# ScalarE's share of magnitudes and scales in an attention and two-layer kernel: sums for v, layer 2's magnitude, one factor folded

## The chip, the cores and the metric

The kernel runs on one core of a Trainium2 chip. The metric is the device time of one execution in microseconds (us), the median of the runs; lower is better.

## The reference

Four batches of eight heads (sequence 576, head size 64) go through a masked softmax attention; its output is a 2304 x 512 matrix x, which passes through two dense layers, each with its own pair of weights (512 x 2048 and 2048 x 512):

```python
scores = np.where(masks, scale * q @ k.T, -1e9)      # heads 0-3: a band of 32; heads 4-7: every 32nd
x = softmax(scores) @ v                              # 2304 x 512
h = x @ moe_w_in;  g = np.maximum(0.01 * h, h);      x = g @ moe_w_out
h = x @ moe2_w_in; g = np.maximum(h, 0) + np.log1p(np.exp(-np.abs(h)))
return g @ moe2_w_out
```

The weights arrive as 64-bit floats and are turned into numbers on the chip.

## The kernel before

Every operand of a dense product is split into two f16 parts, a high part and what is left of it, and one product becomes three matmuls (`mm3`, L453 to L456). To be split, a matrix is scaled by a power of two that comes from a bound of its magnitude. So each weight quarter runs through a chain: load (SP's DMA queue, L147), magnitude (`largest`, VectorE, L156), spread over the partitions (`over`, one TensorE product, L122), factors (`scale`, VectorE), integer work on the two words (`low` L162, `sign` L198, VectorE), `shift` (ScalarE, L204), `merge` (VectorE, L209), `high` (ScalarE, L219) and `rest` (L224, GpSimd or VectorE). For w_out of layer 1 (`plan_together`) one more ScalarE pass, `fold` (L216), multiplies the merged quarter by its factor `by` before the split.

Attention works batch by batch in six halves. `dots` (L314) makes scores, `top` finds their maxima (VectorE, L331 for batch 0, L337 otherwise), `expo` (ScalarE, L360) the exponentials with their sums, `guard` and `norm` (L368 to L377) the reciprocals, `spread` (GpSimd, L382) multiplies, `turn` (L391) transposes, `fetch` (ScalarE, L399) copies out of PSUM, `pv` (L411) multiplies by v, and `high` and `rest` (L439 to L450) write x as two f16 parts. The scale of x comes from `largest` over v (VectorE, L257) with `over` and `factor`.

Layer 1 runs over eight token groups of 288: `gate1` makes h in PSUM (L454 to L456), ScalarE bends and splits it (L475, L478), GpSimd makes the rest (L481), and w_out follows. Layer 2 runs over nine groups (`Unit`) of 256 tokens and eight k each. For each k, `first` makes h; `size` takes its magnitude by clearing the sign bit (VectorE, L1124); `relu` (ScalarE, L1131) reads the same h and frees its PSUM bank; `soft` is an exponential with the scale `nsc` and a logarithm (ScalarE, L1138, L1139); `add` joins them (GpSimd, L1143); `sums` (VectorE, L1151), `cut_high` (ScalarE, L1155) and `cut_rest` (VectorE, L1159) make the operands of `second`.

The order on each engine is not written out. Steps are given to `Plan` with an engine, an estimated cost, what they depend on, the buffers that they take and free, and a rank; `Plan.run` lets each engine take, among the steps that can start within 0.5 us of the earliest, the one of smallest rank. `RANKS` holds two numbers for each kind of step: an offset and a slope. Each engine works through its own list in order, SP's queue of loads too. Up to 130 us of planned time, `Plan` fills planned holes of TensorE with products that nobody reads (`idle`, L92, "fillers" below), which keep the engine active.

Of the kernel before, what the change touches and what calls it, by code (L numbers as in the profile page):

```python
# [9 lines left out]
BF16 = mybir.dt.bfloat16  # L10
F16 = mybir.dt.float16
F32 = mybir.dt.float32
I32 = mybir.dt.int32
U32 = mybir.dt.uint32
U16 = mybir.dt.uint16
AF = mybir.ActivationFunctionType
# [4 lines left out]
P = 128  # L21
# [34 lines left out]
def build(tc, qt, kl, ks, v, wi1, wo1, wi2, wo2, mloc, mstr, out):  # L56
    nc = tc.nc
    with ExitStack() as ctx:
# [82 lines left out]
        class Weight:  # L141
# [73 lines left out]
            def fold(self, q, by):  # L215
                nc.scalar.activation(self.f[q], self.f[q], AF.Copy, scale=by)  # L216

            def high(self, q, hl):
                nc.scalar.activation(flat(hl[0]), self.f[q], AF.Copy)  # L219
                self.hl[q] = hl  # L220

            def rest(self, q, eng):
                hi, lo = self.hl[q]
                eng.tensor_tensor(out=flat(lo), in0=self.f[q], in1=flat(hi), op=ALU.subtract)  # L224

# [6 lines left out]
        class Attn:  # L232
# [22 lines left out]
            def largest(self):  # L255
# [3 lines left out]
                )  # L259

# [378 lines left out]
        def plan_attention(A, ld, after=(), behind=(), scaled=()):  # L639
# [8 lines left out]
            big = step("DVE", 3.05, lambda half: A.largest(), [ld["v"]], 1)  # L648
# [43 lines left out]
        def plan_together(W, name, after, parts, then, w1):  # L692
# [28 lines left out]
            for q in range(4):  # L721
                y = step("ACT", 2.07, lambda q=q: W.shift(q, st["s"]), [t] + read[q], 4 + q)
                y = step("DVE", 2.2, lambda q=q: W.merge(q), [y], 4 + q, port=True)
                y = step("ACT", 1.8, lambda q=q: W.fold(q, O1.by[:, q : q + 1]), [y], 4 + q)
                y = step("ACT", 1.85, lambda q=q: W.high(q, parts(q)), [y] + made[-1:] * (q % 2), 4 + q)
# [602 lines left out]
```

## Time and profile before

| | |
|---|---|
| median of 3 runs | 862.68 us (861.14 to 863.2) |
| the profiled execution, its own time | 861.51 us |
| its span in the trace | 859.7 us |
| mean granted clock of TensorE | 0.995 |
| busy: TensorE, VectorE, ScalarE, GpSimd | 834.1, 552.7, 499.7, 289.4 us |

Busy time counts the fillers for TensorE. What the kernel can win is TensorE's time without a product that counts: its idle time, its fillers, and products at the lower clock. A number like "L257" is a line of the kernel before; lines of the changed kernel are some 19 to 24 higher past line 260.

### The profile page before, as it was taken

The page shows a single profiled execution, that of the slowest core. Times are in us where ns is not written, and L with a number is a line of the kernel's source. Part 1 is how long each engine was busy: PE and PEld are TensorE (multiplying, and loading weights), DVE is VectorE, ACT ScalarE, POOL GpSimd, SP SyncE. Part 2 cuts the span into 40 slices and gives each one's busy share as a digit, 9 for nine tenths or more (in the row PEclk, how much of TensorE's full clock was granted, in tenths as well). Part 3 has the DMA queues.
Part 4 walks back from the last instruction along what each step waited for, and adds up shares of the span by engine and source line. Part 5 has one row for each costly group of instructions (what it writes and reads, how often), then busy time and mean ns, then how long its engine had stood idle before and what let it go on. Part 6 is the DMA issues. An engine that isn't in the chain of part 4 may idle for free.

```text
span 859.7 us, 17683 instructions
## 1 busy us (share of the span) xinstructions
PE 834.1 (97%) x7353; PEld 686.2 (80%) x7353; DVE 552.7 (64%) x1236; ACT 499.7 (58%) x934; POOL 289.4 (34%) x198
## 2 busy tenths in 40 slices
PE   9979999999999999999999999999999999999997
PEld 5547677778777777788877787888888888888886
DVE  4999794534305360038757869877787878776675
ACT  4766969835655241354626367556575656566573
POOL 2457747702242041221605033313222322222131
PEclk9989999999999999999999999999999999999999
DMA  9833320231104540022221120000000000000000
GB/s 369 360 111 128 143 99 1 75 131 57 43 17 181 197 196 2 1 98 100 98 99 29 70 99 1 25 2 27 1 26 1 26 1 26 25 2 25 2 25 26
DMA packets 10992, 63.28 MB, mean 74 GB/s; under 512 B 1344, under 2 KB 1440, under 8 KB 7840
## 3 DMA queue, kind: packets, MB, share of 16 engines
q1 hardware_dynamic: 10656, 62.00, 19.1%
q8 instruction: 57, 0.93, 0.4%
q14 instruction: 23, 0.19, 0.1%
q10 hardware_dynamic: 256, 0.16, 0.1%
HBM read 57.44 MB, written 4.72 MB: 72 GB/s over the span
## 4 chain that ended last, share of the span: by engine, by line
PE 63%; DVE 18%; ACT 7%; DMA 5%; issue 4%; POOL 3%; DVEq 0%; POOLq 0%; ACTq 0%
PE h L454 10%; PE h L456 10%; PE h L455 10%; PE o L454 10%; PE o L456 10%; PE o L455 10%; DMA pair<-wo_dram 3%; DVE pair L198 3%; DVE gr L1159 2%; ACT pair L204 2%; PE ps L314 2%; DVE pair L162 2%; POOL w L224 2%; DVE pair L209 2%; DVE m L156 1%
## 5 line engine op out<-in xcount | busy, mean ns | idle before, releaser
L456 PE MATMUL h<-x,w 128*128 128x256 f16 (+1 forms) x1088 | 304.4, 280 | 6.6 <-POOL w L224 6.6
L454 PE MATMUL h<-x,w 128*128 128x256 f16 (+1 forms) x1088 | 304.5, 280 | 4.6 <-ACT t L475 1.9
L455 PE MATMUL h<-x,w 128*128 128x256 f16 (+1 forms) x1088 | 304.4, 280 | 0.0
L1143 POOL TENSOR_TENSOR pair<-pair,t 128x512 f32<-128x512 f32 x72 | 98.8, 1372 | 271.4 <-ACT t L1139 173.6
L481 POOL TENSOR_TENSOR g<-t,g 128x576 f16<-128x576 f32 x64 | 105.1, 1648 | 159.7 <-ACT g L478 159.6
L456 PE MATMUL o<-g,pair 128*128 128x288 f16 x512 | 146.4, 286 | 0.4 <-POOL pair L224 0.3
L454 PE MATMUL o<-g,pair 128*128 128x288 f16 x512 | 146.5, 286 | 0.0
L455 PE MATMUL o<-g,pair 128*128 128x288 f16 x512 | 146.4, 286 | 0.0
L456 PEld LDWEIGHTS <-w 128*128 128x128 f16 x1088 | 106.8, 98 | 26.7 <-POOL w L224 7.2
L455 PEld LDWEIGHTS <-w 128*128 128x128 f16 x1088 | 106.8, 98 | 23.9 <-issue 4.8
L454 PEld LDWEIGHTS <-w 128*128 128x128 f16 x1088 | 106.8, 98 | 21.2 <-ACT w L219 1.0
L1155 ACT ACTIVATE gr<-pair,x2b 128x896 f16<-128x896 f32 x72 | 73.9, 1040 | 63.6 <-DVE pair L1151 63.6
L1159 DVE SCALAR_TENSOR_TENSOR gr<-pair,x2b,gr 128x896 f16<-128x896 f32 x72 | 86.4, 1211 | 27.4 <-ACT gr L1155 26.9
L1151 DVE TENSOR_TENSOR pair<-pair 128x128 f32<-128x128 f32 x288 | 78.3, 316 | 20.2 <-POOL pair L1143 17.7
L382 POOL TENSOR_TENSOR s<-s,sm 96x512 f32<-96x512 f32 (+3 forms) x48 | 49.7, 1055 | 113.4 <-DVE sm L377 72.5
L1131 ACT ACTIVATE pair<-h,x2s 128x512 f32<-128x512 f32 x72 | 49.1, 682 | 60.3 <-DVE t L1124 57.5
L454 PE MATMUL o<-w,gr 128*128 128x256 f16 x306 | 83.4, 273 | 0.0
L456 PE MATMUL o<-w,gr 128*128 128x256 f16 x306 | 83.4, 273 | 0.0
L455 PE MATMUL o<-w,gr 128*128 128x256 f16 x306 | 83.4, 273 | 0.0
L475 ACT ACTIVATE t<-h,gs 128x576 f32<-128x576 f32 x64 | 47.2, 737 | 59.8 <-PE h L456 59.8
L1124 DVE TENSOR_SCALAR t<-h 128x512 int32<-128x512 int32 x72 | 49.2, 685 | 32.0 <-PE h L456 31.3
L456 PEld LDWEIGHTS <-pair 128*128 128x128 f16 x512 | 50.0, 98 | 13.8 <-POOL pair L224 1.2
(123 smaller groups left out, 1396.5 us busy)
## 6 DMA issues: line engine op xcount, KB each, us to landing
pair<-wo_dram SPq DMA_DIRECT2D x12, 2048.0 KB, 7.8
pair<-wi_dram SPq DMA_DIRECT2D x8, 2048.0 KB, 11.0
out_dram<-pair SPq DMA_DIRECT2D x18, 256.0 KB, 2.2
q<-qt_dram SPq DMA_DIRECT2D x12, 288.0 KB, 4.3
v<-v_dram SPq DMA_DIRECT2D x2, 1408.0 KB, 14.9
pair<-v_dram SPq DMA_DIRECT2D x2, 1408.0 KB, 6.5
k<-ks_dram SPq DMA_DIRECT2D x7, 288.0 KB, 3.5
k<-kl_dram SPq DMA_DIRECT2D x5, 304.0 KB, 3.7
```

The source lines that it names most:

```text
L382: nc.gpsimd.tensor_tensor(out=sv, in0=sv, in1=rs, op=ALU.mult)
L454: nc.tensor.matmul(ps, ah, bh, start=first, stop=False)
L455: nc.tensor.matmul(ps, ah, bl, start=False, stop=False)
L456: nc.tensor.matmul(ps, al, bh, start=False, stop=last)
L475: nc.scalar.activation(t, ps, AF.Prelu, scale=gates[f // 4], alpha=0.01)
L481: nc.gpsimd.tensor_tensor(out=g[:, 1, f : f + 2, :], in0=t, in1=g[:, 0, f : f + 2, :], op=ALU.subtract)
L1124: nc.vector.tensor_scalar(out=t.bitcast(I32), in0=self.ps[k].bitcast(I32), scalar1=0x7FFFFFFF, scalar2=None, op0=ALU.bitwise_and)
L1131: nc.scalar.activation(r[:, :4].rearrange("p (j h) n -> p j (h n)", j=2), self.ps[k], AF.Relu, scale=self.sc[:, k // 2 : k // 2 + 1],)
L1143: nc.gpsimd.tensor_tensor(out=r, in0=r, in1=self.a[k], op=ALU.add)
L1151: nc.vector.tensor_tensor(out=r[:, o], in0=r[:, x], in1=r[:, y], op=op)
L1155: nc.scalar.activation(self.a[k][:, 0], self.r[k][:, 1:], AF.Copy, scale=self.ag)
L1159: nc.vector.scalar_tensor_tensor(out=a[:, 1], in0=self.r[k][:, 1:], scalar=self.ag, in1=a[:, 0], op0=ALU.mult, op1=ALU.subtract)
```

## The change

1. For batches 0 and 1 the bound of v is no longer a maximum by VectorE but a sum of magnitudes by ScalarE: `sums` makes two passes of 1408 elements with a Prelu of slope -1 and its accumulated sum, and `larger_sum` (VectorE) takes the larger of the two. The passes write their unread result into the place that later holds the third quarter's parts of w_in, so that quarter's split waits for them.
2. For w_out of layer 1 the pass `fold` is gone: its factor goes into the scale of `high` (ScalarE) and into `rest_of`, which moves the rest from GpSimd to VectorE.
3. In layer 2 `size` moves from VectorE to ScalarE: a Prelu of slope -1 that also applies the scale, so that the exponential has the fixed scale -1 and `nsc` is not made any more. `size` now also waits for `scales`.
4. Every number of `RANKS` is new, so the order changes on all engines.

```diff
 RANKS = {
-    "A0": (593.918, 6.350), "A1": (1468.724, 0.341), "A2": (1303.427, 4.470), "A3": (216.970, 32.247),
...
+    "A0": (680.119, 0.623), "A1": (395.941, 0.229), "A2": (1137.495, 3.336), "A3": (-67.134, 0.062),
...
-            def fold(self, q, by):
-                nc.scalar.activation(self.f[q], self.f[q], AF.Copy, scale=by)
-
-            def high(self, q, hl):
-                nc.scalar.activation(flat(hl[0]), self.f[q], AF.Copy)
+            def high(self, q, hl, by=1.0):
+                nc.scalar.activation(flat(hl[0]), self.f[q], AF.Copy, scale=by)
...
+            def rest_of(self, q, by):
+                hi, lo = self.hl[q]
+                nc.vector.scalar_tensor_tensor(
+                    out=flat(lo), in0=self.f[q], scalar=by, in1=flat(hi), op0=ALU.mult, op1=ALU.subtract
+                )
...
+            def sums(self):
+                n = self.vf.shape[1] // 2
+                self.m2 = sml.tile([P, 2], F32, name="m2", tag="vm2")
+                junk = wpa.tile([P, 4 * QW], BF16, name="junk", tag=f"a{self.b}3")
+                for i in range(2):
+                    nc.scalar.activation(
+                        junk[:, :n], self.vf[:, i * n : (i + 1) * n], AF.Prelu, alpha=-1.0,
+                        accum_out=self.m2[:, i : i + 1],
+                    )
+
+            def larger_sum(self):
+                self.m = sml.tile([P, 1], F32, name="m", tag="vm")
+                nc.vector.tensor_reduce(out=self.m, in_=self.m2, axis=AX.X, op=ALU.max)
...
-            big = step("DVE", 3.05, lambda half: A.largest(), [ld["v"]], 1)
+            if b < 2:
+                A.read = step("ACT", 2.8, lambda half: A.sums(), [ld["v"]], 1)
+                big = step("DVE", 0.1, lambda half: A.larger_sum(), [A.read], 1)
+            else:
+                big = step("DVE", 3.05, lambda half: A.largest(), [ld["v"]], 1)
...
-                y = step("ACT", 1.8, lambda q=q: W.fold(q, O1.by[:, q : q + 1]), [y], 4 + q)
-                y = step("ACT", 1.85, lambda q=q: W.high(q, parts(q)), [y] + made[-1:] * (q % 2), 4 + q)
-                made.append(step("Pool", 4.1, lambda q=q: W.rest(q, nc.gpsimd), [y], 4 + q))
+                y = step("ACT", 1.85, lambda q=q: W.high(q, parts(q), O1.by[:, q : q + 1]), [y] + made[-1:] * (q % 2), 4 + q)
+                made.append(
+                    step("DVE", 2.3, lambda q=q: W.rest_of(q, O1.by[:, q : q + 1]), [y], 4 + q, port=True)
+                )
...
-        w1 = [plan_quarter(W1, "W1", q, q, [], in_a, [], gate_scale, "Pool") for q in range(4)]
+        w1 = [plan_quarter(W1, "W1", q, q, [], in_a, [A.read, A1.read] * (q == 3), gate_scale, "Pool") for q in range(4)]
...
             def size(self, k):
                 t = self.a[k] = tmp.tile([P, 2, U1], F32, name="t", tag="t")[:, :, :U2]
-                nc.vector.tensor_scalar(
-                    out=t.bitcast(I32), in0=self.ps[k].bitcast(I32), scalar1=0x7FFFFFFF, scalar2=None, op0=ALU.bitwise_and
-                )
+                nc.scalar.activation(t, self.ps[k], AF.Prelu, scale=self.sc[:, k // 2 : k // 2 + 1], alpha=-1.0)
...
-                nc.scalar.activation(a, a, AF.Exp, scale=self.nsc[:, k // 2 : k // 2 + 1])
+                nc.scalar.activation(a, a, AF.Exp, scale=-1.0)
...
-                size = plan.add("DVE", 0.6, bind(U.size), [g1], rank("Fd", k), take=["t"])
+                size = plan.add("ACT", 0.6, bind(U.size), [g1, scaled], rank("Fa", k), take=["t"])
```

What the change moves shows at three places. The first is the start of SP's queue of loads (with buffer numbers; `v0_127` and `v1_130` are the buffers of v of batches 0 and 1, whose tails also hold q and k). Before:

```order
L245 DMA v0_127<-qt_dram 128x576
L246 DMA v0_127<-kl_dram 128x608
L245 DMA v1_130<-qt_dram 128x576
L246 DMA v1_130<-kl_dram 128x608
L252 DMA v0_127<-v_dram 128x2816
L245 DMA v0_127<-qt_dram 128x576
L246 DMA v1_130<-ks_dram 128x576
L245 DMA q_178<-qt_dram 128x576
L246 DMA k_179<-ks_dram 128x576
L147 DMA pair0_125<-wi1_dram 128x4096 x2
```

The same place now (`v1_127` is the buffer of batch 1's v, `v0_131` that of batch 0):

```order
L255 DMA v1_127<-v_dram 128x2816
L248 DMA v0_131<-qt_dram 128x576
L249 DMA v0_131<-kl_dram 128x608
L248 DMA v1_127<-qt_dram 128x576
L249 DMA v1_127<-kl_dram 128x608
L255 DMA v0_131<-v_dram 128x2816
L248 DMA v0_131<-qt_dram 128x576
L249 DMA v1_127<-ks_dram 128x576
L248 DMA q_210<-qt_dram 128x576
L249 DMA k_211<-ks_dram 128x576
L248 DMA q_215<-qt_dram 128x576
L249 DMA k_216<-kl_dram 128x608
```

The load of v of batch 1, the eighteenth load before, is now the first, and a pair of q and k of batch 1 stands ahead of the first quarter of w_in.

The second place is the start of ScalarE's list. Before:

```order
L78 ACT_TABLE_LOAD
L97 DMA ml<-mloc_dram 96x512
L98 DMA ms<-mstr_dram 128x234
L360 ACTIVATE s,sm<-ps,mx 96x128 x16
L399 ACTIVATE a<-pt 128x384 x2
```

Now:

```order
L78 ACT_TABLE_LOAD
L97 DMA ml<-mloc_dram 96x512
L98 DMA ms<-mstr_dram 128x234
L271 ACTIVATE junk,m_134<-v_127 128x1408 x2
L271 ACTIVATE junk,m_206<-v_131 128x1408 x2
L379 ACTIVATE s,sm<-ps,mx 96x128 x16
L418 ACTIVATE a<-pt 128x384 x2
```

The sums of both batches stand ahead of the first exponentials.

The third place is ScalarE's list around the first quarter of w_in (`shift` of `pair_125`, then its `high` into `w`; `s` with `s,mx` are exponentials of batch 1). Before:

```order
L441 ACTIVATE x<-po 128x2x18x7 x2
L399 ACTIVATE a<-pt 108x432 x2
L204 ACTIVATE pair_125<-pair_125,s 128x2048
L441 ACTIVATE x<-po 128x2x18x6 x2
L399 ACTIVATE a<-pt 108x216 x2
L219 ACTIVATE w<-pair_125 128x2048
```

Now:

```order
L460 ACTIVATE x<-po 128x2x18x7 x2
L204 ACTIVATE pair_125<-pair_125,s 128x2048
L418 ACTIVATE a<-pt 108x432
L379 ACTIVATE s,sm<-s,mx 96x128 x4
L418 ACTIVATE a<-pt 108x432
L460 ACTIVATE x<-po 128x2x18x6 x2
L418 ACTIVATE a<-pt 108x216
L379 ACTIVATE s,sm<-s,mx 96x128 x4
L418 ACTIVATE a<-pt 108x216
L216 ACTIVATE w<-pair_125 128x2048
```

Eight exponentials of batch 1 now run between the shift and the split of that quarter. On TensorE, the list ahead of the first product of layer 1 holds 92 fillers in place of 73, two more halves of batch 1's `dots` and two more groups of four transposes; behind that product there are 10 fillers in place of 30. In all there are 102 fillers in place of 103.

## Rows read from the trace of the kernel before

**Rows 1.** The page, busy us, share of the span and instructions by engine.

```profile
PE 834.1 (97%) x7353; PEld 686.2 (80%) x7353; DVE 552.7 (64%) x1236; ACT 499.7 (58%) x934; POOL 289.4 (34%) x198
```

**Rows 2.** Stretches: from:to, length, busy us (instructions) by engine, PEclk, DMA share, GB/s.

```profile
0.00:13.00 13.00, 11.38 (x62) 5.41 (x62) 4.79 (x5) 4.16 (x17) 0.70 (x6) 1.00 0.88 331
0.00:50.70 50.70, 41.31 (x329) 23.74 (x330) 37.69 (x71) 30.82 (x113) 20.64 (x19) 0.98 0.76 309
50.70:130.00 79.30, 74.95 (x658) 56.01 (x659) 69.78 (x188) 57.84 (x160) 50.19 (x30) 0.97 0.36 130
130.00:200.00 70.00, 68.71 (x585) 54.46 (x583) 32.55 (x79) 46.77 (x76) 37.11 (x19) 1.00 0.18 63
450.00:600.00 150.00, 145.32 (x1280) 124.91 (x1279) 120.67 (x209) 94.77 (x121) 49.41 (x30) 1.00 0.10 36
600.00:800.00 200.00, 200.00 (x1834) 179.38 (x1833) 150.51 (x356) 123.55 (x172) 51.49 (x41) 1.00 0.04 14
800.00:859.70 59.70, 53.83 (x494) 48.02 (x491) 38.85 (x89) 31.58 (x44) 12.90 (x10) 0.98 0.05 19
```

**Rows 3.** Waits of TensorE: total us, times, longest us.

```profile
PE h L456 <- POOL w L224: 6.6, 2, 5.6
PE po L411 <- DVE x L450: 2.1, 1, 2.1
PE h L454 <- ACT t L475: 1.9, 2, 1.0
PE h L454 <- ACT pair L1131: 1.8, 1, 1.8
```

**Rows 4.** Timeline of TensorE at the first products: start, us, engine, line.

```profile
50.70 0.42 PE L456 MATMUL h<-x,w 128*128 128x288 f16 x1 [5.64 <-POOL w L224]
...
55.17 0.29 PE L454 MATMUL h<-x,w 128*128 128x288 f16 x1
```

**Rows 5.** Groups by line, shapes apart: fillers, dots, transposes; busy us, mean ns, idle before.

```profile
L92 PE MATMUL idle<-idb 128*128 128x512 bf16 x103 | 28.7, 404 | 1.6 <-DVE idb L83 1.6
L391 PE MATMUL pt<-ident,s 96*128 96x96 f32 x96 | 12.4, 251 | 0.9 <-ACT a L399 0.8
L314 PE MATMUL ps<-k,q 64*96 64x128 f32 x120 | 8.7, 281 | 0.0
```

**Rows 6.** Timeline of ScalarE: first exponentials, shift and split of w_in's first quarter.

```profile
9.74 0.36 ACT L360 ACTIVATE s<-ps,mx 96x128 f32<-96x128 f32 x1 [7.73 <-DVE mx L344]
10.10 0.35 ACT L360 ACTIVATE s<-ps,mx 96x128 f32<-96x128 f32 x1
...
38.10 2.22 ACT L204 ACTIVATE pair<-pair,s 128x2048 f32<-128x2048 f32 x1 [0.43 <-DVE pair L198]
...
42.67 1.91 ACT L219 ACTIVATE w<-pair 128x2048 f16<-128x2048 f32 x1 [0.71 <-DVE pair L209]
```

**Rows 7.** Timeline of VectorE: maximum of v, merge of w_in's first quarter.

```profile
10.97 3.07 DVE L257 TENSOR_REDUCE m<-v 128x1 f32<-128x2816 f32 x1
...
40.35 2.29 DVE L209 SCALAR_TENSOR_TENSOR pair<-pair 128x2048 int32<-128x2048 int32 x1 [0.38 <-ACT pair L204]
```

**Rows 8.** Timeline of GpSimd: the rests of w_in's first two quarters.

```profile
44.66 5.99 POOL L224 TENSOR_TENSOR w<-pair,w 128x2048 f16<-128x2048 f32 x1 [5.77 <-ACT w L219]
...
58.51 4.09 POOL L224 TENSOR_TENSOR w<-pair,w 128x2048 f16<-128x2048 f32 x1
```

**Rows 9.** Groups of layer 2 by line: busy us, mean ns of one, idle before.

```profile
L1155 ACT ACTIVATE gr<-pair,x2b 128x896 f16<-128x896 f32 x72 | 73.9, 1040 | 63.6 <-DVE pair L1151 63.6
L1138 ACT ACTIVATE t<-t,x2n 128x512 f32<-128x512 f32 x72 | 51.1, 710 | 0.6 <-DVE t L1124 0.6
L1131 ACT ACTIVATE pair<-h,x2s 128x512 f32<-128x512 f32 x72 | 49.1, 682 | 60.3 <-DVE t L1124 57.5 <-DVE gr L1159 1.8
L1124 DVE TENSOR_SCALAR t<-h 128x512 int32<-128x512 int32 x72 | 49.2, 685 | 32.0 <-PE h L456 31.3
L1139 ACT ACTIVATE t<-t 128x512 f32<-128x512 f32 x72 | 45.4, 630 | 2.3
```

More of the change, by code (lines that the diff above doesn't have):

```diff
@@ L1097, in scales @@
                 new = lambda n, t: sml.tile([P, n], F32, name=t, tag=t)
-                self.sc, self.nsc = new(4, "x2s"), new(4, "x2n")
+                self.sc = new(4, "x2s")
                 nc.vector.tensor_scalar(
@@ L1101, in scales @@
                 )
-                nc.vector.tensor_scalar(out=self.nsc, in0=self.sc, scalar1=-1.0, scalar2=None, op0=ALU.mult)
                 t = new(4, "x2b")
```

18 rows, old and new, of the table RANKS are left out of this document.

## The prediction

> **What bounds the kernel now.** The page's busy times come first: TensorE is busy 834.1 of 859.7 us, VectorE 552.7 and ScalarE 499.7 [rows 1]. So an engine that is made faster gains only what TensorE loses today, and that is read from the stretches, then from TensorE's waits. Idle is length less busy: 9.4 us up to the first full product of layer 1 at 50.7, 4.3 from there to 130, 1.3 up to 200, 4.7 between 450 and 600, none between 600 and 800, 5.9 at the end [rows 2]. VectorE is the fullest engine beside TensorE from 0 to 130 (107 of 130 us), so it sets the pace of the front; between 450 and 600 it is busy 121 of 150. The waits name the holes: 6.6 us for the rest of a w_in quarter on GpSimd, 2.1 for x's low part, 1.9 and 1.8 for ScalarE passes that free PSUM banks [rows 3]. Behind the longest hole the clock is down: a product takes 0.42 us at 50.70 and 0.29 again at 55.17 [rows 4]; the granted clock went from the 2.4 to the 1.2 GHz level after the 5.64 us without work, so about half of 4.4 us, 2.2, is lost. The fillers are busy 28.7 us more [rows 5], but their number stays (103, then 102). With the products unchanged, the result is therefore read as change of idle time plus change of clock loss.
>
> **The front, up to the first product.** Two forces pull apart. *Later:* v of batch 1 (1408 KB, 1.44 MB) now goes ahead of all, and ScalarE sums both v before any exponential. The queue moved 331 GB/s x 13 us = 4.3 MB by 13 us [rows 2]; the new order needs both v (2.88 MB), four pieces of q and k (1.21) and the masks (0.16), 4.25 MB, before batch 0's v is there, so about 13 to 14 us. A pass of 128x1408 has no row; between 682 ns for 512 elements [rows 9] and 1.91 us for 2048 [rows 6] a line gives 1.4 us. Its bounds are those two rows; I take 1.4, since the cost of the passes grows evenly with size (1.04 for 896). Two passes on batch 0's v end near 16.8, and the first exponential, at 9.74 before [rows 6], starts 7.1 us later. *Earlier:* VectorE no longer spends 3.07 us on the maximum of v at 10.97 [rows 7], which held the third set of maxima and so ScalarE; and two copies of about half a us each now stand behind the shift of the first quarter. So that shift (L204), at 38.10 before, starts at 38.1 + 7.1 - 3.1 - 1.0 = 41.1; the bounds are 39, if other holes of ScalarE close as well because its work then waits in line, and 42. Behind it come 2.2 us of shift, eight exponentials (0.36 apart [rows 6], 2.9), four copies and two x parts (some 2.3), then the split, 1.9: 50.4. VectorE's merge (2.29 [rows 7]) fits under the exponentials. GpSimd's rest took 5.99 us for this quarter and 4.09 for the next [rows 8]; I take 4.1, as VectorE's neighbours there are now maxima and small steps, not the long integer passes; 5.99 is the bound. The first full product starts at **54.5**, bounds 52.4 and 57.3; that is 3.8 later than 50.7.
>
> The Trainium skill, SBUF — State Buffer, section "Who interferes with whom", says that a VectorE instruction with two SBUF inputs, or in a two-port mode, keeps GpSimd waiting. By that rule the place would go to 5.99 wherever such passes meet the rest, and the gain of the front would shrink by 1.9 us. The trace has both durations [rows 8], but not which neighbour made the difference.
>
> What TensorE does before and behind that point is counted from the lists. Moved ahead: two halves of `dots`, 32 of the trace's matmuls at 8.7/120 us, 2.3; eight transposes at 12.4/96, 1.0 [rows 5]. Gone behind it: 20 fillers at 28.7/103, 5.6 [rows 5]. In their place batch 1's tokens with the first two quarters fill the time in which the third quarter is still worked on. Net: 3.8 - 2.3 - 1.0 - 5.6 = **-5.1 us**; with the bounds, -7.2 to -2.3. The hole before the first product shrinks but does not close, so I take half of the clock loss as saved: **-1.1** (0 to -2.2).
>
> **50 to 200 us.** VectorE loses the second maximum of v (3.07 us) as well. Idle there is 4.3 us [rows 2], partly the 2.1 us wait for x's low part. But attention and products are now interleaved more closely, and each transpose or product with v waits for a chain over three engines; I take 0, with 4 either way. For w_out, ScalarE loses four folds (a pass of this size takes 1.91 [rows 6], 7.6 in all) and GpSimd four rests (about 4.1 each [rows 8]), while VectorE gains four `rest_of`; the nearest row is the merge, the same instruction over the same shape, 2.29 [rows 7], so 9.2 us, on an engine that is busy 33 of 70 us there [rows 2]. A quarter is ready 1.9 + 4.1 - 2.3 = 3.7 us sooner. Of the 1.3 us idle I take **-0.5** (0 to -1.3). If VectorE were full there, the 9.2 us would show on the path.
>
> **Layer 2.** VectorE gives up 72 passes of 685 ns, ScalarE gains 72; the nearest row is `relu`, same shape, same source, 682 ns [rows 9]: 49 us change hands. In 600 to 800 this is worth nothing, since TensorE is busy 200.00 of 200 [rows 2]. Between 450 and 600, VectorE also prepares w_out of layer 2, and 3.7 of the 4.7 us are waits behind ScalarE [rows 3]. The 1.8 us wait for `relu`, whose own wait was for `size` on VectorE (57.5 of its 60.3 us idle [rows 9]), should go; the 1.9 us behind L475 are ScalarE's own and stay [rows 3]. I take **-2.0** (0 to -4.7).
>
> The Trainium skill, ScalarE: Activation LUTs, section "Rules for kernel authors", speaks against this move: relu and max belong on VectorE, not ScalarE. Here 685 ns on VectorE stand against 682 on ScalarE [rows 9], f32 out of PSUM, so the trace does not bear out a price for it; the sum by the rule would put the steady part at ScalarE's pace, which is the first rival.
>
> **Sum.** -5.1 - 1.1 + 0 - 0.5 - 2.0 = -8.7 against the profiled execution's own 861.51: 852.8. The median of the runs stands 1.17 above that execution, so **854.0**. The bounds of the terms, which do not all fall on one side, give 849 to 859 as this case's own range.
>
> **Rivals.**
>
> *ScalarE sets the pace of layer 2 (slower).* TensorE makes four first products in a row; one takes 24 x 200/1834 = 2.6 us [rows 2], one second part 2.3. With two PSUM banks, the sixth first product of a group can start only when the fourth's `relu` is done. From the end of the second to that start there are 10.2 us. ScalarE has in that time three each of size and relu (4.1), three pairs of exponential and logarithm (4.0) and two cuts (2.1): 10.2 by their durations [rows 9], some 9.5 as far as neighbours overlap. A second place like it comes two products later. If each is late by d, nine groups lose 18 d: from 0.5 us on the whole gain is gone, at 1 us the time is 854 + 18 = 872. For it: the margin is thin. Against it: ScalarE is busy 124 of 200 us there [rows 2], 150 with the added passes less overlap, and the exponential without its per-partition scale should cost nearer to the logarithm's 630 than 710 ns. Chance 0.18.
>
> *The front gives it back (no change).* VectorE or GpSimd stays the last to finish: the rest takes 5.99 again, the first product comes at 57 or later, and the closer interleaving adds 4 us of short waits. -2.3 + 4 - 2.5 = -0.8, near 862. For it: 9.4 of the 25.6 idle us lie ahead of the first product, at the end of that one chain [rows 2]. Chance 0.14.
>
> *Nearly all holes close (faster still).* No clock loss (-2.2), front -7.2, 450 to 600 without waits (-4.7): -14, near 848. For it: VectorE sheds 6 us in the front and 0.7 per k later. Chance 0.10.
>
> My forecast keeps 0.58. That the moved work is simply hidden holds for the steady part of layer 2 and is in the sum.
>
> **How the numbers follow.** A measurement tells 0.3% (2.6 us) from no change: below 860.1 counts as faster, above 865.3 as slower. Faster: forecast, the better rival and a fifth of the no-change case, 0.70. Same: most of the no-change case, 0.13. Slower: ScalarE's pace, 0.17. The range reaches from 846.5, which takes in most of the better case, to 866, into the first rival: four fifths.
>
> **What would show it.** Right: the first full product near 54.5 with fewer fillers behind it; less than 20 us idle on TensorE in all; L224 of the first quarter near 4.1; no wait for w_out's rests; 600 to 800 still without idle time on TensorE. Wrong: waits of TensorE for L1152 (`relu`) in every group of layer 2; a first product at 57 or later; more than 9 us idle between it and 130.

## The result and the profile after

The changed kernel takes 853.33 us (median of 3 runs, 853.30 to 853.89) where 854.0 was forecast; the ratio to the kernel before is 0.9896 (95% interval 0.9877 to 0.9915), which is 9.0 us less; the two medians lie 9.3 apart. The profiled execution took 853.89 us, with a span of 852.1; the span of before is 859.7. Executions of one kernel spread by some 5 us (860.0 to 866.0 for the kernel before, the longer ones mostly at a lower mean granted clock), so that a ratio below is known to 1 to 3 us and a difference under some 2 us is not told from none.

The page of the kernel after, busy times, beside [rows 1]:

```profile
PE 831.7 (98%) x7352; PEld 684.8 (80%) x7352; DVE 507.0 (59%) x1159; ACT 533.8 (63%) x1010; POOL 274.6 (32%) x194
```

The span is 7.6 shorter: TensorE is idle 20.4 us in place of 25.6 (-5.2), and busy 2.4 less, mostly time at the lower clock. The stretches of the kernel after (columns as in [rows 2]) show where:

```profile
0.00:54.50 54.50, 48.49 (x391) 28.38 (x392) 34.30 (x127) 41.23 (x156) 20.67 (x21) 1.00 0.76 299
54.50:130.00 75.50, 72.36 (x654) 55.65 (x654) 65.62 (x123) 57.42 (x134) 58.50 (x33) 1.00 0.37 133
130.00:200.00 70.00, 68.02 (x601) 54.37 (x600) 45.56 (x105) 40.37 (x83) 21.31 (x13) 1.00 0.17 59
450.00:600.00 150.00, 146.70 (x1300) 126.77 (x1299) 108.42 (x199) 107.96 (x149) 43.12 (x30) 1.00 0.10 36
600.00:800.00 200.00, 200.00 (x1835) 179.37 (x1833) 126.74 (x309) 144.58 (x213) 52.60 (x40) 1.00 0.04 14
```

Length less busy: 6.0 us up to 54.5 (before 9.4), 3.1 to 130 (before 4.3 by the row below), 2.0 to 200 (1.3), 3.3 between 450 and 600 (4.7), none in 600 to 800, 5.9 at the end as before. The same second stretch of the kernel before, which no group shows:

```profile
54.50:130.00 75.50, 71.15 (x643) 53.62 (x642) 65.98 (x187) 56.17 (x160) 50.19 (x30) 1.00 0.34 125
```

TensorE's first products in the kernel after (timeline, beside [rows 4]):

```profile
54.40 0.30 PE L475 MATMUL h<-x,w 128*128 128x288 f16 x1 [1.12 <-POOL w L221]
54.53 0.29 PE L473 MATMUL h<-x,w 128*128 128x288 f16 x1
```

The first full product is at 54.40, 54.5 forecast. The hole ahead of it is 1.12 us and not 5.64, and the products behind it take 0.29 at once: the clock stayed at its 2.4 GHz level, where the products before had 4.4 us at the 1.2 GHz level [rows 4]. The granted clock of 0 to 54.5 went from 0.94 to 1.00.

The chain of the first quarter, from the timelines of ScalarE and GpSimd after, beside [rows 6, 8]:

```profile
13.41 1.38 ACT L271 ACTIVATE junk<-v 128x1408 bf16<-128x1408 f32 x1 [3.26 <-DMA v<-v_dram]
...
39.58 2.19 ACT L204 ACTIVATE pair<-pair,s 128x2048 f32<-128x2048 f32 x1 [0.50 <-DVE pair L198]
...
48.27 2.04 POOL L401 TENSOR_TENSOR s<-s,sm 96x512 f32<-96x512 f32 x2 [6.18 <-DVE sm L396]
50.27 4.08 POOL L221 TENSOR_TENSOR w<-pair,w 128x2048 f16<-128x2048 f32 x1
```

The split (L216) runs from 47.80 to 49.7; the rest begins at 50.27, when GpSimd is through with two softmax multiplications that stand ahead of it.

The waits of TensorE after, beside [rows 3]:

```profile
PE o L475 <- DVE gr L1180: 2.1, 2, 1.4
...
PE pm L122 <- DVE m L732: 1.3, 1, 1.3
...
PE h L473 <- ACT pair L1152: 0.5, 2, 0.3
```

Nothing waits for a rest of w_out, and `relu` (L1152) is waited for twice, 0.5 us in all. What this cannot tell is which of the three pieces of work, or the new order, earned the time. That is what the runs ask.

### The profile page after: what moved, and what is told of

It reads as the page before. It is cut to its first block, busy times and chain, and to the rows that moved or that the text cites. A ratio compares the mean times of both kernels' runs of the same rounds, so it can differ in the third digit from the quotient of the medians.

```text
span 852.1 us, 17667 instructions
## 1 busy us (share of the span) xinstructions
PE 831.7 (98%) x7352; PEld 684.8 (80%) x7352; DVE 507.0 (59%) x1159; ACT 533.8 (63%) x1010; POOL 274.6 (32%) x194
## 4 chain that ended last, share of the span: by engine, by line
PE 77%; DVE 9%; ACT 6%; DMA 3%; issue 2%; POOL 2%; DVEq 0%; POOLq 0%; ACTq 0%; SPq 0%
PE o L473 12%; PE o L475 12%; PE o L474 12%; PE h L473 11%; PE h L475 11%; PE h L474 11%; PE idle L92 2%; DMA pair<-wo_dram 2%; PE ps L333 2%; DVE pair L198 2%; PE pt L410 2%; PE po L430 2%; DVE pair L209 1%; ACT s L379 1%; ACT pair L204 1%
## 5 line engine op out<-in xcount | busy, mean ns | idle before, releaser
L475 PE MATMUL h<-x,w 128*128 128x256 f16 (+1 forms) x1088 | 303.4, 279 | 1.1 <-POOL w L221 1.1
L1164 POOL TENSOR_TENSOR pair<-pair,t 128x512 f32<-128x512 f32 x72 | 96.3, 1342 | 272.5 <-ACT pair L1152 145.1
L500 POOL TENSOR_TENSOR g<-t,g 128x576 f16<-128x576 f32 x64 | 109.4, 1718 | 171.9 <-ACT g L497 169.4
L475 PE MATMUL o<-g,pair 128*128 128x288 f16 x512 | 146.4, 286 | 0.0
L475 PEld LDWEIGHTS <-w 128*128 128x128 f16 x1088 | 106.4, 98 | 21.9 <-POOL w L221 1.6
L401 POOL TENSOR_TENSOR s<-s,sm 96x512 f32<-96x512 f32 (+3 forms) x48 | 52.3, 1110 | 115.2 <-DVE sm L396 100.3
L475 PE MATMUL o<-w,gr 128*128 128x256 f16 x306 | 83.4, 273 | 0.8 <-DVE gr L1180 0.8
L494 ACT ACTIVATE t<-h,gs 128x576 f32<-128x576 f32 x64 | 47.1, 736 | 56.9 <-PE h L475 54.9
L1147 ACT ACTIVATE t<-h,x2s 128x512 f32<-128x512 f32 x72 | 48.7, 677 | 50.3 <-PE h L475 50.3
L156 DVE TENSOR_REDUCE m<-pair 128x1 f32<-128x2048 f32 x16 | 36.5, 2279 | 41.1 <-DMA pair<-wo_dram 30.6
L475 PEld LDWEIGHTS <-pair 128*128 128x128 f16 x512 | 50.1, 98 | 12.8
```

Of the source, the lines that this page charges most:

```text
L156: nc.vector.tensor_reduce(out=m, in_=hi.bitcast(F32), axis=AX.XY, op=ALU.max, apply_absolute_value=True)
L401: nc.gpsimd.tensor_tensor(out=sv, in0=sv, in1=rs, op=ALU.mult)
L475: nc.tensor.matmul(ps, al, bh, start=False, stop=last)
L494: nc.scalar.activation(t, ps, AF.Prelu, scale=gates[f // 4], alpha=0.01)
L500: nc.gpsimd.tensor_tensor(out=g[:, 1, f : f + 2, :], in0=t, in1=g[:, 0, f : f + 2, :], op=ALU.subtract)
L1147: nc.scalar.activation(t, self.ps[k], AF.Prelu, scale=self.sc[:, k // 2 : k // 2 + 1], alpha=-1.0)
```

## The experiments

In all but four of the runs (the ranks alone, and the three with a table of their own) the order is **held**: the planner keeps the costs and engines that it had, so that the sequence of steps stays the same, and only the instruction that a step emits is another, on another engine at the same place. The medians stand beside about 861.5 for the kernel before, measured along with them. Differences in us below are differences of ratios times 861.5.

| run | order | work | us | ratio (95%) |
|---|---|---|---|---|
| before | old | old | 861.5 | 1 |
| after | new | new | 853.33 | 0.9896 (0.9877 to 0.9915) |
| n_new_order_old_work | new | old | 866.67 | 1.0049 (1.0035 to 1.0063) |
| n_old_order_new_work | old | new | 864.80 | 1.0026 (1.0012 to 1.0040) |
| n_old_order_size_moved | old | size moved | 860.57 | 0.9980 (0.9962 to 0.9998) |
| e4_max_held | new | v's maxima back | 854.40 | 0.9905 (0.9881 to 0.9930) |
| e3_size_held | new | size back | 857.44 | 0.9938 (0.9917 to 0.9960) |
| e5_fold_held | new | w_out back | 861.68 | 0.9992 (0.9978 to 1.0005) |
| e5b_fold_pass_rest_on_vector | new | fold back only | 859.60 | 0.9976 (0.9962 to 0.9990) |
| n_extra_scalar_pass | new | one more pass | 875.71 | 1.0166 (1.0136 to 1.0196) |
| e1_ranks_only | new ranks, own order | old | 915.06 | 1.0594 (1.0560 to 1.0629) |
| t_old_work_new_table | own | old | 875.61 | 1.0148 (1.0111 to 1.0185) |
| t_new_work_new_table | own | new | 856.47 | 0.9940 (0.9917 to 0.9964) |
| t_v_first_rest_on_vector | own | new and two edits | 854.90 | 0.9918 (0.9898 to 0.9939) |

### The ranks alone

The kernel before with the new table and no other edit:

> The kernel before with the new table of ranks alone; both magnitudes of v stay on VectorE, the size of layer 2 stays on VectorE, the w_out fold stays on ScalarE with its rest on GpSimd. Theory (the new order is the gain of the front; the moved work only relieves engines that stand beside it): most of the 9.3 us comes with the order, 856 to 860, with the first full product at 55 to 58 (VectorE pays 3.07 us for one or both maxima) and between 450 and 600 about the 4.7 us idle of before. Rival (the moved passes are the gain, the order only fits them): 862 or more, with the longest wait of TensorE again behind the rest of a w_in quarter and above 3 us.

915.06 us, which neither theory had: 6% slower than before. A stretch of this run:

```profile
130.00:200.00 70.00, 49.93 (x393) 38.18 (x390) 36.98 (x100) 54.38 (x101) 45.37 (x25) 0.80 0.22 83
```

TensorE is idle 20 of 70 us in 130 to 200, at a granted clock of 0.80. A rank only says who goes first among the steps that are ready; with other steps or durations the same ranks make another sequence. So this run says nothing on the new order, only that a table can't be moved to other work. From here on orders were held.

### One piece undone at a time, the new order held

The bounds of v by VectorE again:

```diff
             def sums(self):
...
-                for i in range(2):
-                    nc.scalar.activation(
...
+                self.largest()
...
             def larger_sum(self):
-                nc.vector.tensor_reduce(out=self.m, in_=self.m2, axis=AX.X, op=ALU.max)
+                pass
```

> The changed kernel with the bound of v of the first two batches back as VectorE's absolute maximum (3.07 us each) in the places of the sums; all orders held. Theory (what counts is when the exponentials start and VectorE is free again): batch 1's maximum falls into VectorE's idle time before 10.2 us and costs nothing, batch 0's holds VectorE's steps up to 3 us but lets ScalarE's first exponential start near 13.5 in place of 16.3; so 852.5 to 857, first full product 53.5 to 57.5. Rival (VectorE's path is charged both maxima, 6.1 us): about 859, first full product near 60.

854.40, +0.8 us on the kernel after, inside the theory's range and not told from no difference. VectorE and ScalarE in its timelines:

```profile
7.17 3.09 DVE L260 TENSOR_REDUCE m<-v 128x1 f32<-128x2816 f32 x1 [5.60 <-DMA v<-v_dram]
...
13.91 0.36 ACT L369 ACTIVATE s<-ps,mx 96x128 f32<-96x128 f32 x1 [11.89 <-DVE mx L353]
```

One maximum falls into VectorE's idle time; the exponentials start at 13.91 and not, as in the kernel after, at 16.29; the first full product comes at 55.18, 0.8 later.

Layer 2's magnitude on VectorE again, and with it the exponential's per-partition scale and the step that makes `nsc`:

```diff
-                nc.scalar.activation(t, self.ps[k], AF.Prelu, scale=self.sc[:, k // 2 : k // 2 + 1], alpha=-1.0)
+                nc.vector.tensor_scalar(out=t.bitcast(I32), in0=self.ps[k].bitcast(I32), scalar1=0x7FFFFFFF, scalar2=None, op0=ALU.bitwise_and)
...
-                nc.scalar.activation(a, a, AF.Exp, scale=-1.0)
+                nc.scalar.activation(a, a, AF.Exp, scale=self.nsc[:, k // 2 : k // 2 + 1])
```

> The changed kernel with layer 2's magnitude back on VectorE in the place where it stands now, with its negated scales; all else and all orders held. Theory (moving the size gave 1.4 us between 450 and 600 and nothing where TensorE is busy throughout): 854 to 855.5, with 600 to 800 still 199.9 or more of 200 busy on TensorE and VectorE back to about 150 of 200. Rival (layer 2's move is a main part of the gain): 857 or more, with idle time of TensorE spread over all of layer 2.

857.44, +3.6: above the theory's range and at the rival's lower end, though the place is the theory's. Its stretches and waits, and a product of TensorE's timeline:

```profile
450.00:600.00 150.00, 144.70 (x1268) 124.44 (x1266) 119.57 (x215) 94.91 (x123) 45.11 (x30) 0.99 0.10 36
600.00:800.00 200.00, 200.00 (x1834) 179.23 (x1833) 150.10 (x357) 125.57 (x172) 53.50 (x41) 1.00 0.04 14
...
PE o L475 <- DVE gr L1183: 3.4, 2, 2.1
PE h L474 <- DVE x L1115: 1.7, 1, 1.7
...
515.95 0.42 PE L473 MATMUL o<-w,gr 128*128 128x256 f16 x1
```

600 to 800 stays full with VectorE at 150 of 200. Between 450 and 600 VectorE is 11 us fuller and TensorE idle 5.3 us, now behind VectorE's own work: `cut_rest` (gr) and x of layer 2. Idle time is 2.0 of the 3.4 us between the two profiled spans (855.5 and 852.1); most of the rest is clock: behind the hole of 2.06 us at 514.36 the products ran at the 1.2 GHz level (0.42 us each, as in the last line) until 518.9, worth some 1.7.

w_out's factor as a pass of its own, the rest on GpSimd:

```diff
-            def high(self, q, hl, by=1.0):
-                nc.scalar.activation(flat(hl[0]), self.f[q], AF.Copy, scale=by)
+            def high(self, q, hl, by=None):
+                if by is not None:
+                    nc.scalar.activation(self.f[q], self.f[q], AF.Copy, scale=by)
+                nc.scalar.activation(flat(hl[0]), self.f[q], AF.Copy)
...
-                nc.vector.scalar_tensor_tensor(out=flat(lo), in0=self.f[q], scalar=by, in1=flat(hi), op0=ALU.mult, op1=ALU.subtract)
+                nc.gpsimd.tensor_tensor(out=flat(lo), in0=self.f[q], in1=flat(hi), op=ALU.subtract)
```

> The changed kernel with w_out of layer 1 prepared as before: a pass of its factor on ScalarE (1.9 us), then the rest on GpSimd (4.1 us) in place of VectorE's 2.3 to 3.3 us; all orders held. Theory (each quarter is ready some 3.7 us later, but there is slack behind it): 853.3 to 856, at most the first quarter's product near 148 waits, 1 to 2 us. Rival (the quarters are needed as soon as they are ready): each of the four waits 1 to 2 us, 857 to 861, with TensorE waiting for L225's successor on GpSimd.

861.68, +8.3: the rival, a little beyond its range, in fewer and longer waits than it said. The piece that the prediction had put at 0.5 us gives back nearly the whole gain when it is undone. From TensorE's timeline, the two long holes, and GpSimd's step behind the second:

```profile
144.72 0.28 PE L473 MATMUL h<-x,w 128*128 128x288 f16 x1 [2.27 <-ACT t L494]
...
174.00 0.42 PE L475 MATMUL o<-g,pair 128*128 128x288 f16 x1 [3.98 <-POOL pair L227]
174.22 0.45 PE L473 MATMUL o<-g,pair 128*128 128x288 f16 x1
...
169.90 4.05 POOL L227 TENSOR_TENSOR pair<-pair 128x2048 f16<-128x2048 f32 x1
```

ScalarE's copy of a gate (L494) stands behind the fold; the fourth quarter's rest ends late; and behind that hole the products run at 0.42 to 0.45 us, the 1.2 GHz level, until 178.3, some 2 us more.

To split the 8.3, the fold alone, with the rest left on VectorE (as above, but `nc.vector.tensor_tensor` in the last line):

> The changed kernel with w_out's factor as a pass of its own on ScalarE again (four passes of 2.0 us), but the rests kept on VectorE; order held. It splits the 8.3 us of the run that also put the rests back on GpSimd. There the trace has 2.3 us behind ScalarE's copy of a gate, 4.0 us behind GpSimd's rest of the fourth quarter (split done at 169.55, rest at 169.90 for 4.05), and some 2 us of lower clock behind that hole. Theory A (both pieces count): the 2.3 us stay, the fourth quarter is ready 1.8 us sooner so that its hole shrinks to about 2 and the clock stays up: 856 to 858.5. Rival B (only the time of the folds on ScalarE counts): 860 to 862. Rival C (only GpSimd's slower rest counts): 853 to 855.

859.60, +6.9: above theory A, just under rival B's range. The four folds on ScalarE are the larger part; GpSimd's slower rest would be 1.4 of the 8.3, which is not told from none. Theory A let the last hole shrink to 2; it is still 3.71. ScalarE and VectorE in their timelines:

```profile
164.78 2.01 ACT L217 ACTIVATE pair<-pair,by_o 128x2048 f32<-128x2048 f32 x1
166.82 1.91 ACT L218 ACTIVATE pair<-pair 128x2048 f16<-128x2048 f32 x1
...
170.30 0.17 DVE L387 TENSOR_SCALAR sm<-sm 96x8 f32<-96x8 f32 x1 [2.74 <-ACT s L379]
170.62 2.24 DVE L227 TENSOR_TENSOR pair<-pair 128x2048 f16<-128x2048 f32 x1
```

The split is done at 168.7, but the rest stands behind a softmax step of batch 2 on VectorE (L387), which waits 2.74 us for exponentials (L379) that ScalarE makes behind that very split. A wait crossed from one chain into another through the order of a queue; counting durations doesn't see it.

### Order and work apart

All three undone together, in the new order:

> The changed kernel's order of work on every engine, but all three pieces of work back where they were before: both bounds of v by VectorE's maxima, the size of layer 2 on VectorE, the w_out factor as a pass of its own with the rest on GpSimd. The three undone alone cost 1.1, 4.1 and 8.3 us against 853.3. Theory A (they lie in three stretches that don't touch, front, 130 to 200 and 450 to 600, so they add up): 865 to 869, that is slower than the kernel before, with TensorE idle some 6 us in 130 to 200 and 5 in 450 to 600. Rival B (the new order is a gain by itself of the size that the front shows, 4 to 5 us, and the undone pieces share their waits): 857 to 861.

866.67, theory A. The three differences alone sum to 12.7 us (0.8, 3.6, 8.3), together they are 13.2: they add up. And the new order is slower than the old one with the old work (+4.2 us). Its stretches:

```profile
0.00:54.50 54.50, 49.02 (x390) 28.44 (x390) 38.92 (x120) 34.48 (x143) 19.73 (x21) 1.00 0.77 299
50.70:130.00 79.30, 75.54 (x684) 57.42 (x681) 69.13 (x148) 61.87 (x154) 61.68 (x34) 1.00 0.36 130
130.00:200.00 70.00, 61.73 (x530) 48.19 (x532) 38.07 (x87) 44.62 (x70) 35.86 (x16) 0.98 0.17 59
```

Up to 130 us TensorE is idle 8.8 us, in the kernel after 9.2: the front's gain belongs mostly to the order. The same product, the 451st of layer 1's first stage (`h`), starts like this in the kernel before, in this run and in the kernel after (timelines of TensorE):

```profile
137.85 0.29 PE L454 MATMUL h<-x,w 128*128 128x288 f16 x1
132.21 0.29 PE L463 MATMUL h<-x,w 128*128 128x288 f16 x1
130.75 0.29 PE L473 MATMUL h<-x,w 128*128 128x288 f16 x1
```

So 5.6 of the 7.1 us come with the order and the old work. Then 8.3 us are idle in 130 to 200, and the long wait is again GpSimd's rest of the fourth w_out quarter, 4.0 us.

The reverse, the three pieces in the old order:

> The order of work of the kernel before, with all three pieces of work moved as in the change. Theory A (the moved work pays little in the old order, since the holes there have other causes: 5.6 us behind GpSimd's rest of the first w_in quarter, 0 behind w_out's quarters): layer 2 gives 1 to 2 us, the sums 0 to 1.5, w_out 0; 858 to 861. Rival B (the moved work is the gain and the order only carries it): 853 to 856.

864.80, +2.2 on before: both theories missed. The front paid, in the timelines of ScalarE, TensorE and GpSimd:

```profile
11.06 1.38 ACT L274 ACTIVATE junk<-v 128x1408 bf16<-128x1408 f32 x1
...
15.47 0.59 PE L331 MATMUL ps<-ml,idb 96*96 96x512 bf16 x2 [2.61 <-ACT s L382]
...
53.06 0.42 PE L478 MATMUL h<-x,w 128*128 128x288 f16 x1 [5.64 <-POOL w L224]
...
47.02 5.98 POOL L224 TENSOR_TENSOR w<-pair,w 128x2048 f16<-128x2048 f32 x1 [5.76 <-ACT w L219]
```

In the old order the sums stand between batch 0's exponentials, TensorE waits 2.61 us for a score bank, and the first full product comes at 53.06, 2.4 us later than before [rows 4]. Some 1.7 us of its profiled execution are clock (last section).

Only the size moved, in the old order:

> The order of work of the kernel before, with only layer 2's magnitude moved to ScalarE. Theory A (as the prediction had it: the wait for relu between 450 and 600 goes, nothing else changes): 859 to 860.5, that is 1 to 2.5 us less than before. Rival B (ScalarE's passes then come later than TensorE's need, since the old order was made for the size on VectorE): 862 or more, with waits of TensorE for relu (pair, the L1131 of this order) above 1.8 us in all.

-1.7 us (860.57): theory A's size. Its other claim fell: `relu` is still waited for, 1.8 us in all. With the order new and the size still on VectorE the wait is nearly gone. The waits of this run, then those of the new order with the old work:

```profile
PE h L454 <- ACT pair L1129: 1.8, 2, 1.1
...
PE h L463 <- ACT pair L1145: 0.2, 1, 0.2
```

So the order took that wait away and not the move. What the move took in the old order is the wait for `cut_rest`, 0.8 us before.

### ScalarE's margin in layer 2

```diff
                 a = self.a[k]
+                nc.scalar.activation(a, a, AF.Copy)
                 nc.scalar.activation(a, a, AF.Exp, scale=-1.0)
```

> The changed kernel with one more ScalarE pass per k in layer 2 (128 x 512, about 0.63 us, over the exponential's tile, result unchanged), 72 in all, right behind the exponential. Theory A (the first rival's bookkeeping: 10.2 us from the end of the second product to the sixth's start, ScalarE's work in them some 9.5 us, so about 0.6 us of slack at two places in each of nine groups): three more passes there are 1.9 us, 1.2 over, so 18 x 1.2 = 22 us, 870 to 880, with waits for relu in every group. Rival B (only ScalarE's mean load counts, 145 of 200 us, 23 per 200 more makes 168): 853 to 856.

The pass stands ahead of the exponential and not behind it, with the same length (629 ns). 875.71, +23.3 where theory A had 22. The wait stands in the places that the rival counted, two in each of nine groups, and 600 to 800 is no longer full:

```profile
PE h L473 <- ACT pair L1152: 16.5, 18, 1.3
...
600.00:800.00 200.00, 190.37 (x1725) 168.58 (x1724) 119.35 (x288) 156.05 (x236) 50.04 (x38) 1.00 0.03 12
```

The 18 waits are 1.3 and 0.7 us by turns in most groups, 0.9 on average where 1.2 was forecast, and make 16.5 of the 23.3; that the total comes so near is partly luck, since other waits grew as well. ScalarE is busy 156 of 200 us and yet sets the pace. So the first rival's mechanism is real, and the change stops short of it.

### Other tables

Three tables searched with the planner's own costs, to see whether any order would do. First the old work:

> The kernel before, all its work where it was, with a table of ranks searched for this work (another order of its own; the table of the change gave 915 with this work, its own old one 861.5). Theory A (the moved passes are needed: VectorE keeps two maxima of 3.07 us in the front and the size of layer 2, so the holes before the first product and between 450 and 600 stay in some form): 857 to 862. Rival B (any table made for its work does it, the moved passes are worth little by themselves): 850 to 855, with TensorE idle 20 us or less in all.

875.61, slower than before and outside both theories: the longest waits are `relu` (6.3 us, 6 times) and ScalarE's copy L475 (5.8 us, 3 times). Then the new work:

> The changed kernel with another table of ranks, searched longer for the same work. Theory A (what is left of the holes, 20.4 us, of which about 8 lie in places that no order removes: 1.6 at the start, 5.9 at the end; a further order can close some of the other 6 to 8 and shed fillers): 847 to 852. Rival B (the order is at its limit for this work and a new one only moves the holes): 853 to 858.

856.47, rival B: a product with v waits 4.1 us for x (L465), and 50.7 to 130 runs at a granted clock of 0.96. Last, two edits of the front (`"v": [ld0["v"]]` as a further condition of batch 1's loads, and the first quarter's rest on VectorE), with a table of their own:

> The changed kernel with two edits and a table searched for them: batch 1's v is loaded behind batch 0's, so that ScalarE's two passes on batch 0's v do not wait for 2.88 MB, and the rest of the first w_in quarter is made by VectorE (2.3 us) in place of GpSimd (4.08). Theory A (the front's end is the chain of the first quarter: exponentials from about 11 in place of 16.3 and a rest that is 1.8 us shorter bring the first full product to 50 to 52): 846 to 851. Rival B (the queue and VectorE, 68.6 of 79.3 us busy behind it, take it back): 852 to 857, with waits for VectorE behind the first product.

854.90, rival B by its time. A stretch:

```profile
50.70:130.00 79.30, 69.73 (x645) 54.34 (x643) 72.05 (x175) 65.97 (x163) 54.39 (x33) 0.98 0.29 106
```

The first full product comes at 44.42, 10 us earlier than in the kernel after, and all of it is lost again: 9.6 us idle between 50.7 and 130. VectorE is busy 72 of 79 there, but TensorE's waits are for ScalarE (3.3 us for L418, 3.2 for L494) and GpSimd (2.3 for L401), and not for VectorE as the rival had it. No version here is faster than the kernel after; 854.40 and 854.90 are not told from it.

## Why the prediction was right, and where it was not

**The total** (854.0 against 853.33) and the forecast case held, with its signs: first product at 54.40, no wait for w_out's rests, 600 to 800 full, the first quarter's rest at 4.08. Idle time was 20.4 where "less than 20" was named. None of the signs of a wrong forecast appeared. That the number fits so closely is partly luck. The sum was made for the profiled execution, -8.7, and the two profiled executions differ by 7.6; the median fits because the median of before lies 1.2 above its profiled execution and that of the kernel after 0.6 below. And the terms below miss on both sides.

**The front, -5.1 - 1.1 + 0 for 50 to 130.** Idle time up to 130 fell from 13.75 to 9.15 us, -4.6, and the lower clock behind the hole is gone, worth 2.2: -6.8 against -6.2. The passes over v took 1.38 us (1.4 taken); the shift started at 39.58 (41.1 taken, bounds 39 to 42). The first product is at 54.4 because two errors cancel: the shift came 1.5 us early, and from it to the start of the rest 10.7 us passed in place of 9.3, with GpSimd's two multiplications and a wait of ScalarE in them. The step "half of the clock loss" was mis-sized: the hole shrank to 1.12 us and the whole 2.2 came back. But the cause was given to the wrong half of the change. The prediction counted 3.1 us to VectorE's lost maximum; with the sums out and the maxima back in the new order the kernel takes 0.8 more, not told from none, and the front with all the old work keeps 5.6 of 7.1 us. It is mostly the order that made the front.

**w_out, -0.5.** Here the reasoning failed. The step said that a quarter is ready 3.7 us sooner and bounded its worth by the 1.3 us that TensorE is idle in 130 to 200 before. That bound holds only if the rest of the program stays where it was. The fourth quarter shows it, in the timelines of GpSimd and TensorE of the kernel before:

```profile
166.33 4.07 POOL L224 TENSOR_TENSOR pair<-pair 128x2048 f16<-128x2048 f32 x1 [0.83 <-ACT pair L219]
...
170.45 0.30 PE L456 MATMUL o<-g,pair 128*128 128x288 f16 x1
```

and of VectorE and TensorE of the kernel after:

```profile
163.24 2.97 DVE L225 SCALAR_TENSOR_TENSOR pair<-pair,by_o 128x2048 f16<-128x2048 f32 x1
...
166.27 0.29 PE L475 MATMUL o<-g,pair 128*128 128x288 f16 x1
```

Both are just in time: the rest ends at 170.40 for a product at 170.45, and at 166.21 for the same product (the 147th of these in both) at 166.27. No wait shows in either, so the trace of before has no number for it, and yet the quarter was without slack. The new order brings TensorE there 4.2 us sooner. ScalarE is full on the way, in the kernel after:

```profile
140.00:150.00 10.00, 9.68 (x88) 7.66 (x86) 9.95 (x23) 9.90 (x10) 4.64 (x4) 1.00 0.28 91
150.00:160.00 10.00, 10.00 (x84) 8.00 (x82) 8.73 (x4) 9.58 (x21) 4.23 (x2) 1.00 0.42 144
```

ScalarE is busy 9.90 and 9.58 of 10 us without the folds; the 8 us of folds had no cover. Undone, the piece costs 8.3 us, and the front's gain is given back within 70 us. The term was small, as said, but of the other sign (idle there rose by 0.7), and its meaning was wrong: it isn't a gain of its own but the condition on which the front's is kept. The sum came out because the new order and the new work fit each other; the working had not looked at that.

**Layer 2, -2.0.** Here it failed as well, though idle between 450 and 600 fell by 1.4. The 1.9 us behind ScalarE's L475, which "stay", are what went. They are waits of layer 1's last groups, in TensorE's timeline of the kernel before:

```profile
455.41 0.28 PE L454 MATMUL h<-x,w 128*128 128x288 f16 x1 [0.89 <-ACT t L475]
465.35 0.28 PE L454 MATMUL h<-x,w 128*128 128x288 f16 x1 [0.96 <-ACT t L475]
```

With the size moved in the old order they stay, 1.9 us; the new order removed them. The 1.8 us wait for `relu` shrank to 0.5, but by the order and not by the move, as the runs above show. In exchange `cut_rest` on VectorE, 0.8 before, took 2.1 and ScalarE's `cut` 0.6 more. From its first product to the end layer 2 takes 365.0 us before (from 494.75) and 365.7 after (from 486.44): it gained nothing. What the move does is to pay for the new order, in which layer 2 takes 369.2 with the size on VectorE (from 486.28); in the old order it takes 363.8 with the size moved (from 494.85). In 600 to 800 the move is worth nothing, as said.

The Trainium skill, ScalarE: Activation LUTs, section "Rules for kernel authors", would keep relu and max on VectorE, for its speed in bf16. The passes here are f32 out of PSUM and cost the same on either engine (685 ns before, 677 after, group below and [rows 9]); what the run with one more pass shows against further work on ScalarE is its load, since ScalarE is then 0.9 us late on average at 18 places.

```profile
L1147 ACT ACTIVATE t<-h,x2s 128x512 f32<-128x512 f32 x72 | 48.7, 677 | 50.3 <-PE h L475 50.3
```

**ScalarE as the pace (0.18).** The bookkeeping of 10.2 us with some 0.7 over was exact enough to name the places of the extra pass's waits, and their size within a third. The exponential without its per-partition scale is 629 ns and not 710 [rows 9], which is part of that margin. **The front gives it back (0.14)** is what happens when w_out's piece is left out: 861.68.

What stays open: no run has part 1 or 2 alone in the old order, so how the 2.2 us of the three together split there is read from one timeline only. And only one other order was made for the old work (875.61), so it is not shown that none suits it better than its own.

## What to carry to other kernels

Idle time in the old trace bounds what a faster step gains only while everything ahead of it stays put. When a change pulls one stage forward, cost the next stage's producers anew against the earlier need: here the front's 7 us lasted only because 8 us left a full ScalarE in the stretch behind it, and because layer 2's magnitude left VectorE. To tell order from work, hold the order and change what a step emits; neither half of this change was a gain by itself in these two orders (+4.2 and +2.2 us), the two together were -9.0.

## What was not expected of the hardware

**GpSimd beside VectorE.** In the old order the first quarter's rest takes 5.98 us also when the maximum of v isn't there, beside the shift's uint16 pass on VectorE (timeline of the old order with the new work):

```profile
46.75 2.44 DVE L198 TENSOR_SCALAR pair<-pair 128x2048 uint16<-128x2048 uint16 x1
```

It begins at 47.02, and 5.98 - 4.08 = 1.90 us is about what is left of that pass (2.17 by its recorded end; VectorE's next step starts at 48.98). So the pass was the neighbour, not the reduction; beside softmax maxima in the kernel after it took 4.08. In the kernel after, the same kind of pass starts while GpSimd is in two steps of softmax (L401) and five products of gates (L500):

```profile
120.60 6.66 DVE L198 TENSOR_SCALAR pair<-pair 128x2048 uint16<-128x2048 uint16 x1
```

6.66 in place of 2.44, and TensorE's next wait on that chain, 1.3 us for m (L732), ends at 129.69. GpSimd lost as well: the two steps took 2.84 us there and the five products 8.33, where one alone takes 1.02 (2.04 for two at 48.27) and 1.29 (at 58.84). That is 0.8 + 1.9 = 2.7 us more, about the length of the pass.

The Trainium skill, SBUF — State Buffer, section "Who interferes with whom", says that whoever issues first keeps the shared ports for its whole instruction and that a reduction takes no part. The first case and the harmless reduction agree. In the second the pass, which met a chain of short steps, took 4.2 us more, longer than any one of them, and they lost too; that both lose there is measured, in which order they waited is not.

**The clock.** Behind the holes of 3.98 and 3.71 us in 130 to 175 the products ran at 0.42 to 0.45 us, the 1.2 GHz level, until 178.3, so 3.98 us without work cost some 2 us more. About 2 us without work had no fixed price. The hole before the same product with v is 2.06 us in the kernel before (to 113.58) and 2.07 with the new work in the old order (to 115.99); the first product of `h` behind it, in the one and in the other:

```profile
115.53 0.30 PE L454 MATMUL h<-x,w 128*128 128x288 f16 x1
...
118.56 0.42 PE L476 MATMUL h<-x,w 128*128 128x288 f16 x1
```

The clock was kept in the first; in the second it was granted at 0.50 from 117.2 to 120.6, worth 1.7 us. It was also lost behind 2.06 us with the size back on VectorE (514.36) and behind 2.05 with the maxima back (178.98), and kept behind 2.27 with the folds back (144.72). In the kernel after no hole between two products is longer than 1.65 us, and every stretch up to 800 has a granted clock of 1.00.
